# Dynamic convolution and squared-ReLU feed-forward on one core: the place of VectorE's sums of a finished chunk in each step

## The chip, the cores and the metric

The kernel runs on one core of a Trainium2 chip. The metric is the device time of one execution in microseconds (us); lower is better. TensorE does the matmuls, VectorE and ScalarE the elementwise work, SyncE issues the DMAs; GpSimd does nothing here after the start.

## The reference

Two layers, one behind the other, in fp32. The first is a convolution whose 7 weights are different at every token and head; the second is a feed-forward layer with a squared ReLU.

```python
w = softmax(weight_gen, axis=-1)            # (8, 4096, 8 heads, 7 taps)
x_pad = concat([zeros(B, 6, 192), x], axis=1)
out = einsum('bshk,bskhg->bshg', w, windows_of_7(x_pad))   # 24 channels per head
x = out.reshape(32768, 192)
h = x @ w_in                                # w_in (192, 2048), given as float64
r = maximum(h, 0.0)
return ((r * r) @ w_out).astype(float32)    # w_out (2048, 192), given as float64
```

## The kernel before

**Chunks.** Each of the 128 partitions holds 256 consecutive tokens. A chunk takes 4 of them from every partition, 512 tokens in all, so there are 64 chunks, numbered c = 0 to 63. For a chunk the convolution runs on VectorE (`conv_steps`): a softmax of six small instructions (L195 to L200, its Exp on ScalarE, L197), seven products (L211) and six additions (L216) over 128x768 tiles, and a transpose by 32x32 blocks (L270); two rounds of DMAs through DRAM (L276, L281) complete the transpose. What comes back, `xT`, is split into a high part and a low remainder (`xh` on ScalarE, L235, and `xl` on VectorE, L236), since TensorE multiplies in a shorter format; the weights `W` and `V` are stored in the same two parts.

**Steps.** A chunk passes through NJ = 8 steps, j = 0 to 7, each for 256 of the 2048 hidden columns. In a step TensorE runs `mm1(c, j)` (L296: 18 matmuls of 64 rows, in nine pairs on the two halves of the array), which fills two PSUM banks `ph`. ScalarE takes them with a ReLU (L314), squares in place (L318), and makes the high part `gh` (L322, `high`); VectorE makes the low part `gl` (L326, `low`). Then `mm2_turned` (L370: 10 matmuls for each of the two blocks, 20 in a step) adds them into four PSUM banks `acc0` to `acc3`. It runs LAG = 2 steps behind: TensorE's row in step (c, j) is `mm1(c, j)` and then the second product of two steps earlier. So the last blocks of chunk c-1 are added in step (c, 1), and in step (c, 2) the second product of chunk c begins and writes the same four banks: `ph` has four banks, `acc` the other four, and there is no second set.

**The sums.** Two banks hold the two row halves of one result. `sum_turned` takes the banks out: ScalarE copies `acc2` and `acc0` to SBUF (L378), and VectorE adds `acc3` and `acc1` to the copies (L380, two instructions), and a DMA (L381) moves a part between partitions. Only then may TensorE write the banks again. `store_turned`, in steps 5 and 6 of the same chunk, transposes the result (L389, L391, L392) and sends it out (L398, L403).

**What sets the order.** The order on every engine is that in which the Python code emits instructions. In a step the loop emits: `mm1`, `mm2_turned`, ReLUs and squares; then `late`, the two `low` instructions of the step before; then the list `todo` for this step, in which the convolution of the chunk after the next has been laid out; then `store_turned`; then, if a chunk has just been finished (`done`), `sum_turned`; then the two `high`. `plan_conv` fills `todo`: from step (m-2, 3) on, the 20 items of chunk m's convolution are spread over eight steps (`spread`), so that three of them (an addition, a product, an addition) fall into step (m-1, 1), the step of the sums. For chunk 2 alone the 14 items behind the softmax all fall into step (1, 0). The last chunk, c = 63, has no convolution beside it. It still takes out chunk 62's sums in its step 1, and its own second product runs at the end in another form (L343).

Of the kernel before, what the change touches and what calls it, by code (L numbers as in the profile page):

```python
# [19 lines left out]
def kernel(  # L20
# [27 lines left out]
    NJ = NF // 2  # L48
# [4 lines left out]
    CONV_BEG = 3  # L53
# [30 lines left out]
    def load_group(gi):  # L84
        t0 = gi * TG
        xt = xin.tile([P, TG + HALO, D], F32, name="xt")
        wt = xin.tile([P, TG, H, K], F32, name="wt")
        x_tiles[gi], w_tiles[gi] = xt, wt
        wf = wt.rearrange("p t h k -> p t (h k)")
        if gi > 0:  # L90
            nc.sync.dma_start(out=wf, in_=wg_v[:, t0:t0 + TG, :])
            nc.sync.dma_start(out=xt, in_=x_v[:, t0 - HALO:t0 + TG, :])
            return
        nc.gpsimd.memset(xt[:, 0:HALO, :], 0.0)
        nc.sync.dma_start(out=wf[:, 0:TC, :], in_=wg_v[:, 0:TC, :])
        nc.sync.dma_start(out=xt[:, HALO:HALO + TC, :], in_=x_v[:, 0:TC, :])
        for p0 in range(0, P, PPB):
            nc.sync.dma_start(
                out=xt[p0 + 1:p0 + PPB, 0:HALO, :],
                in_=x_v[p0:p0 + PPB - 1, R - HALO:R, :],  # L100
            )
# [186 lines left out]
    def mm1(c, j):  # L288
        xh, xl = xts[c]["h"], xts[c]["l"]
        two = [ps_h.tile([P, N], F32, name="ph") for _ in range(2)]  # L290
        seq = [(q, xx, k) for q, xx in ((0, xh), (0, xl), (1, xh)) for k in range(ND)]
        for n, (q, xx, k) in enumerate(seq):
            for i in range(2):
                rows = slice(i * D1, (i + 1) * D1)
                w = W[rows, q, j, k * P:(k + 1) * P]
                nc.tensor.matmul(two[i], w, xx[rows, k], start=(n == 0), stop=(n == len(seq) - 1))  # L296
        for i in range(2):
            phs[c, 2 * j + i] = two[i]

    def relu(c, fb):  # L300
        ph = phs.pop((c, fb))
        if c == 0:
            r = gp.tile([P, N], F32, name="gh" if fb < NBUF else "gl")
        else:
            r = gp.tile([P, N], F32, name="rg")
        rgs[c, fb] = r
        if c == NCH - 1:
            nc.scalar.activation(
                r.rearrange("p (t q j) -> p t q j", q=P // Q, j=Q),
                ph.rearrange("p (q t j) -> p t q j", q=P // Q, j=Q),  # L310
                AF.Relu,
            )
        else:
            nc.scalar.activation(r, ph, AF.Relu)  # L314

    def square(c, fb):
        r = rgs[c, fb]
        nc.scalar.activation(r, r, AF.Square)  # L318

    def high(c, fb):  # L320
        gh = ghs[c, fb] = gp.tile([P, N], F32R, name="gh")
        nc.scalar.copy(gh, rgs[c, fb])  # L322
# [33 lines left out]
    def mm2_turned(c, fb):  # L356
        if fb == 0:
            accs[c] = [ps_o.tile([P, N], F32, name=f"acc{t}") for t in range(4)]
        gh, gl = ghs.pop((c, fb)), gls.pop((c, fb))
        j, i = divmod(fb, 2)  # L360
        first, last = fb == 0, fb == NF - 1
        A, B = [(0, 0, gh), (0, 0, gl), (0, 1, gh)], [(2, None, gh), (2, None, gl)]
        seq = B + A if last or first else A + B
        for n, (b, q, g) in enumerate(seq):
            k = sum(1 for m in seq[:n] if m[0] == b)
            for h in range(2):
                rows = slice(h * D1, (h + 1) * D1)
                w = V[rows, fb, P:2 * P] if q is None else V[rows, fb, 2 * P * q:2 * P * q + P]
                fl = dict(start=first and k == 0, stop=last and k == (2 if b == 0 else 1))
                nc.tensor.matmul(accs[c][b + h], w, g[rows], **fl)  # L370
# [3 lines left out]
    def sum_turned(c):  # L374
        acc = accs[c]
        X = works[c] = stage.tile([P, 3, N], F32, name="raw")
        for k, b in ((1, 2), (0, 0)):
            nc.scalar.copy(X[:, k], acc[b])  # L378
        for k, b in ((1, 2), (0, 0)):
            nc.vector.tensor_tensor(out=X[:, k], in0=acc[b + 1], in1=X[:, k], op=ALU.add)  # L380
        nc.sync.dma_start(out=X[0:D1, 2], in_=X[D1:P, 1])  # L381

    def store_turned(c, part):
        X = works[c]
        if part == 0:
            o_sb = op.tile([P, TC, D], F32, name="o_sb", bufs=2)
            Y = stage.tile([P, 2, N], F32, name="raw")
            outs[c] = o_sb, Y
            nc.vector.transpose(Y[:, 0], X[:, 0])  # L389
        else:  # L390
            nc.vector.tensor_tensor(out=X[0:D1, 1], in0=X[0:D1, 1], in1=X[0:D1, 2], op=ALU.add)  # L391
            nc.vector.transpose(outs[c][1][0:D1, 1], X[0:D1, 1])  # L392
        o_sb, Y = outs[c]
        y = Y[:, part].rearrange("p (t q i) -> p q t i" if c < N_PE else "p (q t i) -> p q t i", t=TC, i=Q)
        for e in range(P // Q if part == 0 else D1 // Q):
            d0 = part * P + e * Q
            for q in range(P // Q):
                nc.sync.dma_start(  # L398
                    out=o_sb[q * Q:(q + 1) * Q, :, d0:d0 + Q],
                    in_=y[e * Q:(e + 1) * Q, q],  # L400
                )
        if part:
            nc.sync.dma_start(out=out_v[:, c * TC:(c + 1) * TC, :], in_=o_sb)  # L403
# [3 lines left out]
    def finish(c, t):  # L407
        if c not in outs:
            o_sb = op.tile([P, TC, D], F32, name="o_sb", bufs=2)
            outs[c] = o_sb, stage.tile([P, TC, 2 * D], F32, name="raw") if c > 0 else None  # L410
        o_sb, tmp = outs[c]
        acc = accs[c][t]
        if c == 0:
            nc.scalar.copy(o_sb[:, t, :], acc[:, 0:D])
        else:
            nc.scalar.copy(tmp[:, t, :], acc[:, 0:2 * D])

    def store(c, t0, t1):
        o_sb, tmp = outs[c]
        tsl = slice(t0, t1)  # L420
        if c > 0:
            for h, l in ((slice(0, P), slice(2 * P, 2 * D)), (slice(P, D), slice(D, 2 * P))):
                nc.vector.tensor_tensor(out=o_sb[:, tsl, h], in0=tmp[:, tsl, h], in1=tmp[:, tsl, l], op=ALU.add)
        nc.sync.dma_start(out=out_v[:, c * TC + t0:c * TC + t1, :], in_=o_sb[:, tsl])
# [70 lines left out]
    def at(c, j, f):  # L495
        todo.setdefault((c + j // NJ, j % NJ), []).append(f)

    def spread(fs, c, j0, j1):
        for i, f in enumerate(fs):
            at(c, j0 + (j1 - j0) * i // len(fs), f)  # L500

    def plan_conv(m, a, b):
        spread(a, max(m - 2, 1), CONV_BEG if m > 2 else 0, CONV_BEG + (NJ if m > 2 else 0))
        for f in b:
            at(m - 1, NJ - 2, f)

# [4 lines left out]
    for c in range(1, NCH):  # L511
        tail = c == NCH - 1
        for j in range(NJ):
            if j == 0 and c % 2 and (c + 3) // 2 * CPG < NCH:
                load_group((c + 3) // 2)
            if j == CONV_BEG and c + 2 < NCH:
                plan_conv(c + 2, *conv_steps(c + 2, 0))
            if c == 1 and j == 0:
                for t in range(TC):
                    finish(0, t)  # L520
                store(0, 0, TC)
            mm1(c, j)
            fbs = (2 * j, 2 * j + 1)
            done = None
            if len(pend) == LAG or tail and pend:
                c2, j2 = pend.pop(0)
                for fb in (2 * j2, 2 * j2 + 1):
                    mm2_turned(c2, fb)
                done = c2 if j2 == NJ - 1 else None
            for fb in fbs:  # L530
                relu(c, fb)
            for fb in fbs:
                square(c, fb)
            if not tail:
                pend.append((c, j))
            for f in late:
                f()
            late.clear()
            for f in todo.pop((c, j), []):
                f()  # L540
            if c > 1 and j == OUT_STEP:
                store_turned(c - 1, 0)
            if c > 1 and j == OUT_STEP + 1:
                store_turned(c - 1, 1)
            if done is not None:
                sum_turned(done)
            if not tail or j < NJ // 2:
                for fb in fbs:
                    high(c, fb)
                    late.append(lambda c=c, fb=fb: low(c, fb))  # L550
# [44 lines left out]
```

## Time and profile before

| what | value |
|---|---|
| time, median of 3 runs | 2361.75 us (2361.68 to 2362.22) |
| the profiled execution's own time | 2361.66 us |
| its span in the profile | 2359.9 us |
| TensorE matmul busy | 2255.2 us |
| VectorE busy | 1872.7 us |
| ScalarE busy | 1792.9 us |
| DMA queue 1, share of 16 engines | 32.0% |
| granted TensorE clock | 1.00 |

The span is the stretch that the profile sees; the execution's own time is 1.76 us longer. In the views, PE is TensorE's matmul side, PEld its weight loads, DVE VectorE, ACT ScalarE and SPq SyncE's queue. A row of the timeline gives the start, the length, the engine, the line, the operation with output<-input, how many instructions were merged into the row (x2: two back to back), and in brackets how long the engine had been idle before it and what ended that. A row of the waits gives the total, the number and the longest. The chain of waits follows the work back from the last instruction to what released it, and so shows which engine sets the time at each moment.

### The profile page before, as it was taken

To read this page: it belongs to the slowest core of one execution; us is meant where nothing else is said; L and a number is where in the kernel's file an instruction comes from. 1 tells how busy PE (TensorE), PEld (TensorE's weight loads), DVE (VectorE), ACT (ScalarE), POOL (GpSimd) and SP (SyncE) were. 2 spreads that over 40 slices of the span, in tenths; PEclk is the share of its full clock that TensorE was granted. 3 is DMA by queue.
4 is the path that set the end of the run, shared out by engine and by line. 5 is a ranking of instruction groups with operands and counts; after the bars stand their busy time and mean duration, and the time that the engine had idled before them with its cause. 6 is when DMAs were issued, how large, how long until landed. Compare 5 with 4: busy or idle time off the path is not lost.

```text
span 2359.9 us, 50238 instructions
## 1 busy us (share of the span) xinstructions
PE 2255.2 (96%) x19632; PEld 1837.4 (78%) x19632; DVE 1872.7 (79%) x2834; ACT 1792.9 (76%) x3462; POOL 1.7 (0%) x7
## 2 busy tenths in 40 slices
PE   7999999999999999999999999999999999999999
PEld 7777777777777777777777777777777777777777
DVE  8978878778788787787887877878878778788784
ACT  5677877777778777777787777777877777778776
POOL 0000000000000000000000000000000000000000
PEclk9999999999999999999999999999999999999999
DMA  5233233333232332333323333323333233332322
GB/s 162 59 87 95 57 82 84 83 94 80 60 96 77 89 85 55 94 81 87 96 59 80 88 80 94 81 60 95 78 89 85 56 94 80 87 95 60 80 57 50
DMA packets 321390, 191.78 MB, mean 81 GB/s; under 512 B 223752, under 2 KB 280968, under 8 KB 317184
## 3 DMA queue, kind: packets, MB, share of 16 engines
q1 hardware_dynamic: 321152, 188.58, 32.0%
q8 instruction: 153, 2.51, 0.5%
q14 instruction: 85, 0.70, 0.1%
HBM read 106.39 MB, written 49.55 MB: 66 GB/s over the span
## 4 chain that ended last, share of the span: by engine, by line
PE 93%; DVE 5%; ACT 1%; issue 0%; DMA 0%; SPq 0%; DVEq 0%; ACTq 0%
PE acc L370 48%; PE ph L296 42%; DVE pr L216 3%; DVE raw L380 2%; PE acc L334 1%; PE acc L343 1%; PE ph L253 1%; DVE pr L211 0%; DVE gl L326 0%; DMA xt<-in_x_dram 0%; ACT rg L318 0%; ACT gh L322 0%; ACT rg L314 0%; DMA raw<-in_moe_w_in_dram 0%; ACT gh L314 0%
## 5 line engine op out<-in xcount | busy, mean ns | idle before, releaser
L370 PE MATMUL acc<-gh,V 64*128 64x512 f32 x5952 | 1239.1, 388 | 85.6 <-DVE raw L380 85.6
L370 PE MATMUL acc<-gl,V 64*128 64x512 f32 x3968 | 1133.2, 390 | 2.6 <-DVE gl L326 2.6
L370 PEld LDWEIGHTS acc<-gh,V 64*128 64x128 f32 x5952 | 912.8, 184 | 243.2 <-DVE raw L380 129.7
L296 PE MATMUL ph<-xh,W 64*128 64x512 f32 x6144 | 1078.8, 386 | 2.9 <-DVE W L156 1.4
L314 ACT ACTIVATE rg<-ph 128x512 f32<-128x512 f32 x992 | 539.5, 596 | 512.8 <-PE ph L296 512.8
L326 DVE TENSOR_TENSOR gl<-rg,gh 128x512 fp32r<-128x512 f32 x1008 | 643.6, 677 | 265.6 <-ACT gh L322 265.6
L296 PEld LDWEIGHTS ph<-xh,W 64*128 64x128 f32 x6144 | 752.3, 184 | 126.6 <-ACT W L148 2.5
L370 PEld LDWEIGHTS acc<-gl,V 64*128 64x128 f32 x3968 | 715.0, 184 | 77.1 <-DVE gl L326 3.9
L318 ACT ACTIVATE rg<-rg 128x512 f32<-128x512 f32 x1008 | 582.0, 634 | 0.0
L322 ACT CAST gh<-rg 128x512 fp32r<-128x512 f32 x1008 | 576.4, 627 | 2.6 <-PE acc L343 2.6
L296 PE MATMUL ph<-xl,W 64*128 64x512 f32 x3072 | 540.1, 386 | 0.0
L296 PEld LDWEIGHTS ph<-xl,W 64*128 64x128 f32 x3072 | 376.8, 184 | 60.7 <-DVE xl L236 0.4
L211 DVE TENSOR_TENSOR pr<-xt,wt 128x768 f32<-128x768 f32 x448 | 419.1, 948 | 3.3 <-DMA xt<-in_x_dram 1.0
L216 DVE TENSOR_TENSOR pr<-pr 128x768 f32<-128x768 f32 x381 | 360.0, 945 | 0.3
L236 DVE TENSOR_TENSOR xl<-xT,xh 128x512 fp32r<-128x512 f32 x186 | 117.6, 687 | 185.2 <-ACT xh L235 185.2
L235 ACT CAST xh<-xT 128x512 fp32r<-128x512 f32 x186 | 103.0, 626 | 0.0
L380 DVE TENSOR_TENSOR raw<-acc,raw 128x512 f32<-128x512 f32 x124 | 78.9, 673 | 3.0 <-ACT raw L378 3.0
L378 ACT COPY raw<-acc 128x512 f32<-128x512 f32 x124 | 66.3, 595 | 0.0
L270 DVE STREAM_TRANSPOSE xr<-pr 128x768 f32<-128x768 f32 x62 | 60.7, 979 | 2.1
L392 DVE STREAM_TRANSPOSE raw<-raw 64x512 f32<-64x512 f32 x62 | 43.9, 709 | 2.1
L389 DVE STREAM_TRANSPOSE raw<-raw 128x512 f32<-128x512 f32 x62 | 43.7, 704 | 0.0
L391 DVE TENSOR_TENSOR raw<-raw 64x512 f32<-64x512 f32 x62 | 42.0, 677 | 0.0
(46 smaller groups left out, 377.1 us busy)
## 6 DMA issues: line engine op xcount, KB each, us to landing
xT<-xd SPq DMA_DIRECT2D x124, 384.0 KB, 4.9
xt<-in_x_dram SPq DMA_DIRECT2D x31, 1344.0 KB, 6.9
out_dram<-o_sb SPq DMA_DIRECT2D x63, 384.0 KB, 2.4
xd<-xr SPq DMA_DIRECT2D x248, 96.0 KB, 2.0
o_sb<-raw SPq DMA_DIRECT2D x1488, 16.0 KB, 1.8
raw<-raw SPq DMA_DIRECT2D x62, 128.0 KB, 2.5
wt<-in_weight_gen_dram SPq DMA_DIRECT2D x31, 224.0 KB, 3.3
raw<-in_moe_w_in_dram SPq DMA_DIRECT2D x16, 192.0 KB, 4.5
```

Source lines behind the costliest of these rows:

```text
L211: tt(out=dst, in0=src, in1=wk.broadcast_to([P, n, G]), op=ALU.mult)
L216: tt(out=prs[k0], in0=prs[k0], in1=prs.pop(k), op=ALU.add)
L235: nc.scalar.copy(xh, src[k])
L236: tt(out=xl, in0=src[k], in1=xh.bitcast(F32), op=ALU.subtract)
L296: nc.tensor.matmul(two[i], w, xx[rows, k], start=(n == 0), stop=(n == len(seq) - 1))
L314: nc.scalar.activation(r, ph, AF.Relu)
L318: nc.scalar.activation(r, r, AF.Square)
L322: nc.scalar.copy(gh, rgs[c, fb])
L326: nc.vector.tensor_tensor(out=gl, in0=rgs.pop((c, fb)), in1=ghs[c, fb].bitcast(F32), op=ALU.subtract)
L370: nc.tensor.matmul(accs[c][b + h], w, g[rows], **fl)
L378: nc.scalar.copy(X[:, k], acc[b])
L380: nc.vector.tensor_tensor(out=X[:, k], in0=acc[b + 1], in1=X[:, k], op=ALU.add)
```

## The change

Two places of the code change. `sum_turned(done)` is called behind `late` and ahead of the `todo` list, where it stood behind the list and the stores. And the 14 items of chunk 2's convolution are spread over steps (1, 0) to (1, 3), where all stood in step (1, 0).

```diff
     def plan_conv(m, a, b):
-        spread(a, max(m - 2, 1), CONV_BEG if m > 2 else 0, CONV_BEG + (NJ if m > 2 else 0))
+        if m > 2:
+            spread(a, m - 2, CONV_BEG, CONV_BEG + NJ)
+        else:
+            spread(a, 1, 0, NJ // 2)
...
             for f in late:
                 f()
             late.clear()
+            if done is not None:
+                sum_turned(done)
             for f in todo.pop((c, j), []):
                 f()
...
                 store_turned(c - 1, 1)
-            if done is not None:
-                sum_turned(done)
```

The first place, on VectorE, is step (2, 1), the first step with sums; every later chunk to 62 repeats it. `gl<-rg,gh` are the two `low`, `pr` the products and additions of the convolution, `raw<-acc` the sums. Before:

```order
118 L326 TENSOR_TENSOR gl<-rg,gh 128x512 x2
119 L216 TENSOR_TENSOR pr<-pr 128x768
120 L211 TENSOR_TENSOR pr<-xt,wt 128x768
121 L216 TENSOR_TENSOR pr<-pr 128x768
122 L380 TENSOR_TENSOR raw<-acc_800,raw 128x512
123 L380 TENSOR_TENSOR raw<-acc_798,raw 128x512
124 L326 TENSOR_TENSOR gl<-rg,gh 128x512 x2
125 L216 TENSOR_TENSOR pr<-pr 128x768
```

The same place with the change:

```order
118 L326 TENSOR_TENSOR gl<-rg,gh 128x512 x2
119 L380 TENSOR_TENSOR raw<-acc_796,raw 128x512
120 L380 TENSOR_TENSOR raw<-acc_794,raw 128x512
121 L216 TENSOR_TENSOR pr<-pr 128x768
122 L211 TENSOR_TENSOR pr<-xt,wt 128x768
123 L216 TENSOR_TENSOR pr<-pr 128x768
124 L326 TENSOR_TENSOR gl<-rg,gh 128x512 x2
125 L216 TENSOR_TENSOR pr<-pr 128x768
```

The two sums have passed three instructions of the convolution; what stands ahead of and behind the five is as it was. (The numbers behind `acc` only count tiles.)

The second place, on VectorE, is steps (1, 0) to (1, 3), where chunk 2's convolution is laid out anew; `xr<-pr` is its transpose, and `mx`, `wt` begin chunk 3's softmax. Before:

```order
81 L326 TENSOR_TENSOR gl<-rg,gh 128x512 x2
82 L216 TENSOR_TENSOR pr<-pr 128x768
83 L211 TENSOR_TENSOR pr<-xt,wt 128x768
...
88 L211 TENSOR_TENSOR pr<-xt,wt 128x768
89 L216 TENSOR_TENSOR pr<-pr 128x768 x2
90 L270 STREAM_TRANSPOSE xr<-pr 128x4x6x32
91 L156 TENSOR_TENSOR V<-du,V 128x4x128
92 L156 TENSOR_TENSOR V<-du,V 128x4x64
93 L326 TENSOR_TENSOR gl<-rg,gh 128x512 x2
94 L195 TENSOR_REDUCE mx<-wt 128x32
95 L196 TENSOR_TENSOR wt<-wt,mx 128x224
```

The same place with the change:

```order
80 L326 TENSOR_TENSOR gl<-rg,gh 128x512 x2
81 L211 TENSOR_TENSOR pr<-xt,wt 128x768
...
88 L211 TENSOR_TENSOR pr<-xt,wt 128x768
89 L156 TENSOR_TENSOR V<-du,V 128x4x128
90 L156 TENSOR_TENSOR V<-du,V 128x4x64
91 L326 TENSOR_TENSOR gl<-rg,gh 128x512 x2
92 L216 TENSOR_TENSOR pr<-pr 128x768 x2
93 L270 STREAM_TRANSPOSE xr<-pr 128x4x6x32
94 L195 TENSOR_REDUCE mx<-wt 128x32
95 L196 TENSOR_TENSOR wt<-wt,mx 128x224
```

The `low` instructions and the two of `V` come earlier among the convolution's; the instructions ahead of row 94 are the same ones on both sides.

## The prediction

> **What bounds the kernel now.** I read the waits first: which engine stands still, and for whom. The columns are the total in us, the number of waits and the longest.
>
> ```profile
> PE acc L370 <- DVE raw L380: 85.6, 61, 1.4
> PE acc L370 <- DVE gl L326: 2.6, 3, 1.3
> DVE gl L326 <- ACT gh L322: 265.6, 194, 5.9
> ```
>
> TensorE has one wait that repeats: 61 times it stands before the second product until VectorE's sums are done. Beside it stand only three waits for `gl`, at the start. VectorE itself waits for ScalarE, much longer in total, but that is slack. Next the chain of waits through one chunk (start, length, what), which shows what the wait consists of.
>
> ```profile
> 1012.87 2.04 PE ph L296 x18
> 1014.91 2.27 PE acc L370 x20
> 1017.17 1.84 PE ph L296 x17
> 1019.01 0.02 issue
> 1019.03 0.94 DVE pr L216
> 1019.97 0.61 DVE raw L380
> 1020.58 0.04 issue
> 1020.62 2.70 PE acc L370 x19
> 1023.33 2.04 PE ph L296 x18
> ```
>
> Step 1 is 2.04 + 2.27 us of TensorE. In step 2 the first product ends, and the chain goes over to VectorE: an addition of the convolution, then the first sum, then TensorE goes on. The price of it comes from the busy time by stretches (length, PE busy, PEld busy and so on): steps 7 to 1 as three, step 2 by itself, and the next six.
>
> ```profile
> 1003.65:1016.57 12.92, 12.92 (x118) 10.68 (x116) 12.07 (x17) 10.91 (x22) 0.00 (x0) 1.00 0.16 25
> 1016.57:1022.72 6.15, 4.74 (x42) 3.40 (x39) 6.15 (x10) 5.43 (x11) 0.00 (x0) 1.00 0.72 235
> 1022.72:1048.56 25.84, 25.84 (x232) 21.36 (x229) 18.58 (x30) 19.33 (x38) 0.00 (x0) 1.00 0.36 86
> ```
>
> An undisturbed step takes 12.92 / 3 = 25.84 / 6 = 4.307 us, with TensorE never idle and its clock granted at 1.00; the step with the sums takes 6.15, that is 1.843 more. The longest list of the chain confirms it over the whole run:
>
> ```profile
> 113.13 2.70 PE acc L370 x19
> 2182.22 2.70 PE acc L370 x19
> ```
>
> These two are 57 chunks apart, (2182.22 - 113.13) / 57 = 36.30 us a chunk, and 36.30 - 8 x 4.307 = 1.845. So TensorE is the bound in seven steps of eight, and in the eighth VectorE's queue is.
>
> **The change, first part: the sums pass three convolution instructions.** Here is VectorE from the `low` pair ahead of that step's convolution to the pair behind it, and TensorE's and ScalarE's rows that matter beside them.
>
> ```profile
> 1016.09 1.28 DVE L326 TENSOR_TENSOR gl<-rg,gh 128x512 fp32r<-128x512 f32 x2
> 1017.29 0.94 DVE L216 TENSOR_TENSOR pr<-pr 128x768 f32<-128x768 f32 x1
> 1019.90 1.27 DVE L380 TENSOR_TENSOR raw<-acc,raw 128x512 f32<-128x512 f32 x2
> 1021.10 1.27 DVE L326 TENSOR_TENSOR gl<-rg,gh 128x512 fp32r<-128x512 f32 x2
> 1016.74 1.07 ACT L378 COPY raw<-acc 128x512 f32<-128x512 f32 x2
> 1018.61 0.18 PEld L370 LDWEIGHTS acc<-gh,V 64*128 64x128 f32 x1
> 1020.62 0.50 PE L370 MATMUL acc<-gh,V 64*128 64x512 f32 x1 [1.41 <-DVE raw L380]
> ```
>
> The three instructions between the `low` pair and the sums take 1019.90 - 1017.29 = 2.61 us. ScalarE's two copies, which the sums need, run from 1016.74 to 1017.81; the first is done about 1017.33. So with the change VectorE begins the sums at 1017.3 to 1017.4 with almost no wait, and they end at about 1018.0 and 1018.65 (1.27 us for two). TensorE's first weights for the new chunk load at 1018.61, its second matmul needs the first sum at about 1018.7, and the second sum's bank is needed two pairs of matmuls later, 0.45 us on (20 matmuls, ten pairs, take 2.27 us). Spare: about 0.65 us for the first, 0.4 to 0.5 for the second. The whole 1.845 should go.
>
> The program has this case without the convolution already, once: in its last chunk nothing else stands in front of the sums.
>
> ```profile
> 2323.59 1.06 PE L296 MATMUL ph<-xh,W 64*128 64x512 f32 x6
> 2323.53 1.07 ACT L378 COPY raw<-acc 128x512 f32<-128x512 f32 x2
> 2324.15 1.29 DVE L380 TENSOR_TENSOR raw<-acc,raw 128x512 f32<-128x512 f32 x2 [2.98 <-ACT raw L378]
> ```
>
> The first sum starts 0.62 us after the copies do, one copy later, and both are over 2324.15 + 1.29 - 2323.59 = 1.85 us after the step's first matmul. A first product lasts 2.04 us. So taking the banks out fits under it, if VectorE is free.
>
> The Trainium skill, page "Perfetto Trace Analysis", section "Optimization Strategy", reads such a gap another way: the same gap repeating on the engine that should be saturated can mean that there isn't enough PSUM for the next tile. The kernel has indeed no second set of accumulator banks; by that rule an order on VectorE would not help and the time would stay. The last chunk's row speaks against it here: one set is enough.
>
> What is queued behind the sums now: the three convolution instructions, 1.27 us later, and then the `low` pair at 1021.10, whose place does not move, since the same five instructions stand ahead of it. But TensorE will be 1.845 us earlier against VectorE from there on. That pair is used in step 3's second product, which began at 1022.72 + 2.04 = 1024.76 and will begin at 1022.92; its first half is done at about 1021.75. Cover remains: over 1 us. The lead is then eaten by VectorE's waits, in the next four steps:
>
> ```profile
> 1028.13 1.29 DVE L326 TENSOR_TENSOR gl<-rg,gh 128x512 fp32r<-128x512 f32 x2 [1.98 <-ACT gh L322]
> 1032.15 1.29 DVE L326 TENSOR_TENSOR gl<-rg,gh 128x512 fp32r<-128x512 f32 x2 [1.83 <-ACT gh L322]
> 1040.77 1.90 DVE L236 TENSOR_TENSOR xl<-xT,xh 128x512 fp32r<-128x512 f32 x3 [3.01 <-ACT xh L235]
> ```
>
> They are 6.8 us, so 1.845 can be taken out of them and VectorE still waits for ScalarE at step 6, as today. From there to the sums it stands against TensorE as it does today. The next thing to be late would be the `low` pair of step 6:
>
> ```profile
> 1009.37 1.24 DVE L326 TENSOR_TENSOR gl<-rg,gh 128x512 fp32r<-128x512 f32 x2
> 1010.22 0.41 PEld L370 LDWEIGHTS acc<-gl,V 64*128 64x128 f32 x2
> ```
>
> Its first half is done at about 1010.0 and used at 1010.22. It is in time today, and it is bound to the step 6 wait, which stays. ScalarE's order is unchanged. It will reach the Exp (L197) of step 3 earlier than VectorE delivers for it and wait a little there; TensorE does not feel that, since `ph` has four banks and `mm1` writes two. SyncE's order is unchanged too: the sums' DMA (L381) is ready some 2.5 us sooner and its consumer (L391) is in step 6. The transposed block of the convolution is sent out at the same moment while its use in step 6 comes 1.845 sooner:
>
> ```profile
> 1029.99 1.28 SPq L281 DMA_DIRECT2D xT<-xd  x2
> 1040.12 1.66 ACT L235 CAST xh<-xT 128x512 fp32r<-128x512 f32 x3
> xT<-xd SPq DMA_DIRECT2D x124, 384.0 KB, 4.9
> ```
>
> The last of it is issued at about 1031.3 and lands 4.9 us later, at 1036.2; the use moves to 1038.3. Cost nothing, 2 us of cover.
>
> **Second part: chunk 2's convolution is spread.** Cost by instructions: none added. What it may free are TensorE's three waits for `gl`, 2.6 us. What limits it is ScalarE: its queue stands at the Exp of chunk 3 until VectorE has done all of chunk 2's convolution, and that work ahead of L196 is the same.
>
> ```profile
> 87.26 0.39 ACT L197 ACTIVATE wt<-wt 128x224 f32<-128x224 f32 x1 [6.10 <-DVE wt L196]
> 101.83 1.29 DVE L326 TENSOR_TENSOR gl<-rg,gh 128x512 fp32r<-128x512 f32 x2
> 103.32 0.39 PE L370 MATMUL acc<-gl,V 64*128 64x512 f32 x2
> 113.13 0.50 PE L370 MATMUL acc<-gh,V 64*128 64x512 f32 x1 [1.04 <-DVE raw L380]
> ```
>
> ScalarE goes on at 87.26 either way, with the work of the 6.10 us before still to do, so the `low` pair at 101.83 stays where it is; its first half ends at about 102.5, and TensorE uses it at 103.32. TensorE can therefore come forward by 0.8 us at most there. I take 0.8. The ends are 0 (a new wait eats it) and about 3.5 (all three waits and the loads lost with them go, if ScalarE's pause should shrink).
>
> **The sum.** Sixty waits of 1.845 are 110.7. The first of the 61 is shorter by 1.41 - 1.04 = 0.37, so 1.47. The start gives 0.8. Together 113.0. Against the profiled execution's 2361.66 (its span 2359.9 and 1.76 around it; the median of the runs is 0.09 above it) that is 2248.7 us. Ends: all of the start's 3.5 and a wait-free rest give 2246.0, and 1 us below for what the rows round away 2245. If VectorE came to the sums one convolution instruction late (0.87, a third of 2.61), 0.87 - 0.65 = 0.22 would be left of every wait, 13.4 us in all, 2262.
>
> **The rivals.**
>
> *VectorE's lag is carried round.* If the 1.845 us of lead were not eaten by VectorE's waits, the `low` pair of step 6, with 0.2 us to spare, would be late by about 1.6 in each of 61 chunks: 100 us come back, 2349. Between that and my forecast lie all partial cases (a part of the lag carried, 0.3 to 1.5 us per chunk). For it: the margin of 0.2 is the smallest I found, and VectorE is busy 29.0 of what will be 34.45 us. Against it: 6.8 us of waits per chunk. 8%.
>
> ```profile
> 1000.00:1036.30 36.30, 34.89 (x306) 28.32 (x304) 29.04 (x44) 27.91 (x55) 0.00 (x0) 1.00 0.40 104
> ```
>
> *The banks are the limit.* The four banks must be emptied by ScalarE and VectorE in series, whatever stands in the queue. If emptying them took 3.9 us from the first product's start instead of 1.85, the wait would stay: 2361, no change. The last chunk's row excludes this unless the copies come late in mid-run; there they start at 1016.74, as early in the step as at the end. 2%. (This is what the sentence of the Trainium skill's page "Perfetto Trace Analysis" would mean here.)
>
> *Slower.* The sums now wait at the head of VectorE's queue for ScalarE's copies, and the convolution and the next `low` pair wait behind them. In the last chunk that wait was 2.98 us, since VectorE had nothing else. In mid-run VectorE arrives when the first copy is done. If ScalarE fell behind so that the copies came X later, the `low` pair for step 3 would be late by X - 1.3 (used at 1022.92 + 0.22, done at 1021.75), and from X = 3.2 on the loss outweighs the 1.845; at X = 4.5 each chunk loses 3.2 - 1.845 = 1.36, 83 us, 2445. ScalarE has a wait for TensorE in nearly every step, so I see no way to it. 3%.
>
> **How the numbers follow.** The forecast has 87%, the carried lag and its partial cases 8%, no change 2%, slower 3%. A measurement of this kernel can tell 0.2%, 4.7 us, from no change. Nearly all partial cases are faster by more than that: faster 0.95, within 0.2% 0.02, slower 0.03. The range is the forecast's own, 2245 to 2263; what it leaves out are the rivals, 13%, and the rarer tail of the start.
>
> **What would show it.** In the profile after, TensorE's waits for L380 should be gone or near it (below 5 us for 85.6); chunks should follow each other every 34.45 us; VectorE's row of the sums should stand ahead of L216 with an idle time under 0.2 us; its waits at the three rows above should sum to about 5 us; the chain should be TensorE for over 97%. I am wrong if TensorE shows a new wait that repeats 61 times: for `gl` (the first rival), for L380 still (the second), or if VectorE's wait for L378 reaches several us per chunk (the third).

## The result, and the profile after

The changed kernel takes 2248.66 us (median of 4 runs, 2248.49 to 2248.87) against 2361.97 us before (4 runs, one more than in the table above, 2361.68 to 2362.22): a ratio of 0.952, with a 95% interval of 0.9504 to 0.9537, 113.3 us less. The two profiled executions stand at 2361.66 and 2248.87 us, 112.8 apart.

First the busy times of the whole span (the page's first part).

```profile
span 2247.1 us, 50238 instructions
PE 2228.5 (99%) x19632; PEld 1846.3 (82%) x19632; DVE 1877.8 (84%) x2834; ACT 1798.7 (80%) x3462; POOL 1.7 (0%) x7
```

Busy time and instructions of VectorE and ScalarE are the same as before within 0.4%; only the span has shrunk around them. In the chain that ended last, TensorE had 93% of the span before; after, it is nearly all of it:

```profile
PE 97%; DVE 1%; ACT 1%; DMA 0%; issue 0%; SPq 0%; DVEq 0%; ACTq 0%
```

What VectorE and TensorE wait for, after:

```profile
DVE gl L326 <- ACT gh L322: 147.5, 193, 5.9
DVE raw L380 <- ACT raw L378: 3.0, 1, 3.0
PEld acc L370 <- DVE gl L326: 2.1, 3, 0.8
PEld acc L370 <- ACT gh L322: 1.1, 1, 1.1
PE acc L370 <- DVE gl L326: 1.0, 3, 0.4
PE acc L370 <- ACT gh L322: 0.7, 1, 0.7
```

TensorE's row for L380 (85.6 us in 61 waits) is gone altogether. The waits of VectorE's `low` instructions for ScalarE have given up 265.6 - 147.5 = 118 us: that is where the time was taken from. The one wait of the sums that is left, 3.0 us, is the last chunk's, as before. Next one chunk by stretches: the whole of it, step 1, step 2, and the other six.

```profile
965.90:1000.36 34.46, 34.46 (x308) 28.48 (x305) 29.13 (x45) 28.02 (x55) 0.00 (x0) 1.00 0.41 109
965.90:970.21 4.31, 4.31 (x41) 3.56 (x38) 4.31 (x7) 3.16 (x7) 0.00 (x0) 1.00 0.15 23
970.21:974.52 4.31, 4.31 (x42) 3.56 (x39) 4.31 (x7) 4.13 (x9) 0.00 (x0) 1.00 0.68 211
974.52:1000.36 25.84, 25.84 (x232) 21.36 (x229) 20.51 (x33) 20.73 (x41) 0.00 (x0) 1.00 0.41 107
```

Step 2, which took 6.15 us, is now a step like any other, and TensorE is busy for the whole of the 34.46 us. VectorE around the sums, and its waits up to step 6:

```profile
969.72 1.28 DVE L326 TENSOR_TENSOR gl<-rg,gh 128x512 fp32r<-128x512 f32 x2
971.00 1.29 DVE L380 TENSOR_TENSOR raw<-acc,raw 128x512 f32<-128x512 f32 x2
972.20 0.95 DVE L216 TENSOR_TENSOR pr<-pr 128x768 f32<-128x768 f32 x1
...
974.81 1.29 DVE L326 TENSOR_TENSOR gl<-rg,gh 128x512 fp32r<-128x512 f32 x2
...
980.84 1.29 DVE L326 TENSOR_TENSOR gl<-rg,gh 128x512 fp32r<-128x512 f32 x2 [0.97 <-ACT gh L322]
...
983.95 1.29 DVE L326 TENSOR_TENSOR gl<-rg,gh 128x512 fp32r<-128x512 f32 x2 [0.92 <-ACT gh L322]
...
992.56 1.90 DVE L236 TENSOR_TENSOR xl<-xT,xh 128x512 fp32r<-128x512 f32 x3 [3.01 <-ACT xh L235]
```

The sums follow the `low` pair with no idle time noted, and the convolution follows them. (They begin 1.28 us behind the pair, while the instruction behind the sums begins 1.20 us after them: some 0.08 us are a wait too short for the view to note.) The three waits that were 1.98, 1.83 and 3.01 are 0.97, 0.92 and 3.01: the first two have paid, together 1.92 us, and the third has not been touched.

### The profile page after: what moved, and what is told of

Same layout as the page of the kernel before. It is cut to its first block, busy times and chain, and to the rows that moved or that the text cites. A ratio compares the mean times of both kernels' runs of the same rounds, so it can differ in the third digit from the quotient of the medians.

```text
span 2247.1 us, 50238 instructions
## 1 busy us (share of the span) xinstructions
PE 2228.5 (99%) x19632; PEld 1846.3 (82%) x19632; DVE 1877.8 (84%) x2834; ACT 1798.7 (80%) x3462; POOL 1.7 (0%) x7
## 4 chain that ended last, share of the span: by engine, by line
PE 97%; DVE 1%; ACT 1%; DMA 0%; issue 0%; SPq 0%; DVEq 0%; ACTq 0%
PE acc L370 49%; PE ph L296 45%; PE acc L334 1%; PE acc L343 1%; PE ph L253 0%; DVE pr L211 0%; DVE pr L216 0%; DMA xt<-in_x_dram 0%; ACT rg L318 0%; ACT gh L322 0%; DVE gl L326 0%; DVE V L156 0%; DMA raw<-in_moe_w_in_dram 0%; ACT rg L314 0%; ACT gh L314 0%
## 5 line engine op out<-in xcount | busy, mean ns | idle before, releaser
L370 PE MATMUL acc<-gh,V 64*128 64x512 f32 x5952 | 1007.5, 386 | 0.7 <-ACT gh L322 0.7
L296 PE MATMUL ph<-xh,W 64*128 64x512 f32 x6144 | 863.9, 386 | 3.0 <-DVE W L156 1.4
L370 PE MATMUL acc<-gl,V 64*128 64x512 f32 x3968 | 772.8, 386 | 1.0 <-DVE gl L326 1.0
L326 DVE TENSOR_TENSOR gl<-rg,gh 128x512 fp32r<-128x512 f32 x1008 | 644.1, 678 | 147.6 <-ACT gh L322 147.5
L296 PEld LDWEIGHTS ph<-xh,W 64*128 64x128 f32 x6144 | 575.8, 184 | 126.9 <-ACT W L148 2.7
L370 PEld LDWEIGHTS acc<-gh,V 64*128 64x128 f32 x5952 | 557.5, 184 | 118.1 <-ACT gh L322 1.1
L370 PEld LDWEIGHTS acc<-gl,V 64*128 64x128 f32 x3968 | 371.7, 184 | 80.1 <-DVE gl L326 2.1
L296 PE MATMUL ph<-xl,W 64*128 64x512 f32 x3072 | 432.3, 386 | 0.0
L296 PEld LDWEIGHTS ph<-xl,W 64*128 64x128 f32 x3072 | 288.3, 184 | 60.8 <-DVE xl L236 0.4
L380 DVE TENSOR_TENSOR raw<-acc,raw 128x512 f32<-128x512 f32 x124 | 79.9, 687 | 3.0 <-ACT raw L378 3.0
L197 ACT ACTIVATE wt<-wt 128x224 f32<-128x224 f32 x64 | 25.1, 392 | 68.3 <-DVE wt L196 68.3
```

The lines of the kernel that those rows point to most:

```text
L326: nc.vector.tensor_tensor(out=gl, in0=rgs.pop((c, fb)), in1=ghs[c, fb].bitcast(F32), op=ALU.subtract)
```

## The experiments

All kernels but one are the changed kernel with an edit. A ratio is to the kernel before, run beside the kernel named. A cost per chunk below is the difference to the changed kernel's 2248.66 us over 61 chunks. In the kernels with a scratch tile the lines are one higher (L371 is L370, L381 is L380).

**Each part alone.** The first keeps only the sums in front and spreads chunk 2's convolution as before:

```diff
     def plan_conv(m, a, b):
-        if m > 2:
-            spread(a, m - 2, CONV_BEG, CONV_BEG + NJ)
-        else:
-            spread(a, 1, 0, NJ // 2)
+        spread(a, max(m - 2, 1), CONV_BEG if m > 2 else 0, CONV_BEG + (NJ if m > 2 else 0))
```

> Only the sums are moved; chunk 2's convolution stands in step (1, 0) as before. Queue theory (the three convolution instructions ahead of the sums were the wait, the spreading is worth the start alone): about 0.6 us above the changed kernel, which came forward by 0.57 us at the start, so 2249.2 us. Rival (the spreading is needed for the gain, since VectorE would otherwise enter the main loop with a lag that it carries from chunk to chunk): waits for L380 or gl come back in many chunks, 2260 us or more.

Measured: 2248.97 us (2248.90 to 2249.20), ratio 0.9524, 0.9511 to 0.9537. The second keeps only the spreading: the kernel before with the other half of the diff.

> Only chunk 2's convolution is spread over steps (1, 0) to (1, 3); the sums stand behind the convolution as before. Queue theory: 61 waits for L380 as before, 0.6 us less at the start, 2361.4 us. Rival (part of the gain comes from the spreading): below 2360 us.

Measured: 2361.34 us beside 2361.53 of the kernel before, ratio 1.0002, 0.9994 to 1.0011. Its waits:

```profile
PEld acc L370 <- DVE raw L380: 130.3, 122, 2.1
PE acc L370 <- DVE raw L380: 86.2, 61, 1.7
PE acc L370 <- DVE gl L326: 1.0, 3, 0.4
```

The whole of the gain belongs to the sums. The spreading takes TensorE's waits for `gl` at the start from 2.6 to 1.0 us and is worth 0.2 to 0.3 us in the medians, which neither run can tell apart from nothing. The rival that the main loop needs it is out.

**How far in front?** The sums were put behind the first of the three convolution instructions, and behind the second:

```diff
-            if done is not None:
-                sum_turned(done)
-            for f in todo.pop((c, j), []):
+            fs = todo.pop((c, j), [])
+            if done is not None:
+                fs.insert(1, lambda: sum_turned(done))
+            for f in fs:
                 f()
```

> The sums are issued behind the first of the three convolution instructions. Queue theory with a spare of 0.65 us: the sums come 0.87 us later, 0.2 to 0.35 us of wait in each of 61 chunks, 12 to 21 us, 2261 to 2270 us. Rival (no spare: whatever delays the sums is paid in full): 0.87 x 61 = 53 us, 2302 us. Rival (the banks are the limit, not the place in the queue): no difference from the changed kernel, 2249 us.

> The sums are issued behind the second of the three convolution instructions. Queue theory: one more instruction of 0.87 us is paid in full now that the spare is used up, 53 us above the kernel with one ahead, 2314 to 2323 us. Rival (no spare): 2355 us. Rival (banks): 2249 us.

Measured: 2256.78 us with one ahead (2255.46 to 2257.78; ratio 0.9556, 0.9543 to 0.957) and 2308.61 with two (2308.52 to 2308.96; 0.9776, 0.9761 to 0.9791). With three it is the kernel that only spreads, 2361.34. So the three instructions cost 8.1, 51.8 and 52.7 us, or 0.13, 0.85 and 0.86 us per chunk. An instruction takes 0.87 us (2.61 / 3). The second and third are paid in full or nearly so, the first to 0.13: 0.74 us of it cost nothing. That excludes both rivals, no spare (53 us at once) and the banks as the limit (no cost). My expectation for the first, 12 to 21 us, failed: the measured 8.1 is a third below its lower end. I had taken the whole 0.87 us as delay of the sums, but in the changed kernel they wait some 0.08 us for ScalarE's first copy anyway, so they come only 0.79 later, and 0.79 less my spare of 0.65 is 0.14, near the 0.13 that was measured. In the kernel with one ahead no matmul is listed as waiting for the sums. The wait is in the weight loads, and the second product of that step takes 2.40 us for 2.27:

```profile
PEld acc L370 <- DVE raw L380: 14.7, 62, 0.3
```

```profile
1011.15 2.40 PE acc L370 x20
```

**Is VectorE's idle time slack, and where?** One addition over a scratch tile was added in chunks 2 to 62, in step 4 and, in another kernel, in step 6:

```diff
+    junk = const.tile([P, TC * D], F32, name="junk")
...
+            if 1 < c < NCH - 1 and j == 4:
+                nc.vector.tensor_tensor(out=junk, in0=junk, in1=junk, op=ALU.add)
             if c > 1 and j == OUT_STEP:
                 store_turned(c - 1, 0)
```

> One more VectorE addition over a scratch tile of 128x768 (0.87 us from start to start) in step 4 of chunks 2 to 62, behind the convolution's share. Queue theory: VectorE waits 0.92 us for ScalarE right behind it in the changed kernel, and 3 us more up to step 6, so it costs nothing, 2248.7 us. Rival (VectorE's lag is carried round, its waits are no slack): up to 0.87 x 61 = 53 us, 2302 us.

> The same added instruction in step 6, between the splits and the low pair that TensorE uses 0.24 us after it is ready. Queue theory: the place counts, not the amount; 0.87 - 0.24 = 0.63 us in each of 61 chunks, 38 us, 2287 us, with a new wait of TensorE for gl (L326). Rival (VectorE has room anywhere, 5 us per chunk): 2248.7 us.

Measured: 2248.35 us in step 4 (2248.27 to 2249.11), nothing; 2285.73 us in step 6 (2285.48 to 2286.13; ratio 0.9678, 0.9663 to 0.9692), 37.1 us or 0.61 per chunk. The row of step 4, with the wait behind it that was 0.92 us and has vanished:

```profile
1016.87 0.89 DVE L549 TENSOR_TENSOR junk<-junk 128x768 f32<-128x768 f32 x1
1017.87 1.29 DVE L327 TENSOR_TENSOR gl<-rg,gh 128x512 fp32r<-128x512 f32 x2
```

And step 6: VectorE's added instruction and the `low` pair, and TensorE's weight load that waits for that pair, a wait that the changed kernel doesn't have in the main loop.

```profile
1011.69 0.95 DVE L549 TENSOR_TENSOR junk<-junk 128x768 f32<-128x768 f32 x1
...
1013.90 1.24 DVE L327 TENSOR_TENSOR gl<-rg,gh 128x512 fp32r<-128x512 f32 x2
```

```profile
1014.60 0.19 PEld L371 LDWEIGHTS acc<-gl,V 64*128 64x128 f32 x2 [0.74 <-DVE gl L327]
```

```profile
PEld acc L371 <- DVE gl L327: 46.6, 63, 0.8
```

The same 0.87 us of work costs nothing in one step and 0.61 in another, though VectorE is idle about 5 us in each chunk: the lag is not carried round, it is absorbed at the next wait, but between the splits and that `low` pair there is no wait. The spare there is 0.87 - 0.61 = 0.26 us.

**Does waiting at the head of the queue cost?** ScalarE got one, then two copies over a scratch tile in front of its copies of the banks, so that the sums wait at the head of VectorE's queue with the convolution and the next `low` pair behind them:

```diff
             if done is not None:
+                if not tail:
+                    for _ in range(1):
+                        nc.scalar.copy(junk, junk)
                 sum_turned(done)
```

> One more ScalarE copy over a scratch tile of 128x512 (0.52 us from start to start) ahead of the two copies of the accumulators in chunks 2 to 62, so the sums wait 0.5 us at the head of VectorE's queue. Queue theory: inside the spare of 0.5 to 0.7 us, 0 to 5 us, 2249 to 2254 us. Rival (waiting at the head of the queue is dear, since the convolution and the next low pairs wait behind): 0.5 x 61 = 32 us, 2280 us.

> Two such copies, 1.04 us. Queue theory: 0.35 to 0.55 us beyond the spare in each of 61 chunks, 21 to 34 us, 2270 to 2283 us, shown as waits of TensorE for L380, not for gl, since the low pair behind has over 1 us of cover. Rival (the head of the queue is dear): 63 us or more, 2312 us, with waits for gl too.

Measured: 2248.36 us with one (2248.20 to 2249.11) and 2279.10 with two (2279.01 to 2279.32; ratio 0.965, 0.9634 to 0.9666), 0 and 30.4 us, 0.50 per chunk. The row of the sums with one copy:

```profile
1005.46 1.29 DVE L381 TENSOR_TENSOR raw<-acc,raw 128x512 f32<-128x512 f32 x2 [0.52 <-ACT raw L379]
```

With two, the idle time and the waits:

```profile
1019.65 1.29 DVE L381 TENSOR_TENSOR raw<-acc,raw 128x512 f32<-128x512 f32 x2 [1.17 <-ACT raw L379]
```

```profile
DVE raw L381 <- ACT raw L379: 73.9, 62, 3.0
PEld acc L371 <- DVE raw L381: 47.5, 122, 0.5
PEld acc L371 <- DVE gl L327: 2.1, 3, 0.8
```

With one copy VectorE stands still for half a us in every chunk and TensorE feels nothing. With two it stands still for 1.17 us and 0.50 is paid, so 0.67 is spare; the wait is for the sums alone, and the wait for `gl` remains the start's three. What the third rival said, a late `low` pair behind the waiting sums, doesn't show up to this delay; a longer one was not run.

**What of the start is left?** In step (1, 3) ScalarE stands 6.07 us before chunk 3's Exp. The softmax's first instructions were put in front of the rest of chunk 2's convolution:

```diff
             if j == CONV_BEG and c + 2 < NCH:
+                left = todo.pop((c, j), []) if c == 1 else []
                 plan_conv(c + 2, *conv_steps(c + 2, 0))
+                if left:
+                    todo[c, j] += left
```

> The changed kernel, with one order in step (1, 3) turned round: chunk 3's first softmax instructions (L195, L196, and the Exp) ahead of the last three instructions of chunk 2's convolution. Queue theory: ScalarE's wait of 6.07 us for L196 ends 2.8 us sooner, TensorE's waits of 0.73 for gh and 0.42 for gl in the first chunk go and about 0.3 for gl is left: 1 us below the changed kernel, 2247.6 us. Rival (the start is bound elsewhere): 2248.7 us.

> The changed kernel again, on the chip of the run before it, as its measure: 2248.7 us by every theory.

Measured: 2250.73 us (ratio 0.9522, 0.9509 to 0.9535; four runs: 2250.70, 2250.89, 2250.75 and 2248.97) against 2248.63 of the changed kernel on the same chip (2248.56 to 2248.83; 0.9515, 0.9502 to 0.9528). My expectation failed. The rival's holds in one run (2248.97); in the other three something comes on top. ScalarE's row in the changed kernel, and then its rows here:

```profile
87.29 0.39 ACT L197 ACTIVATE wt<-wt 128x224 f32<-128x224 f32 x1 [6.07 <-DVE wt L196]
```

```profile
84.32 0.39 ACT L197 ACTIVATE wt<-wt 128x224 f32<-128x224 f32 x1 [3.23 <-DVE wt L196]
97.01 1.66 ACT L235 CAST xh<-xT 128x512 fp32r<-128x512 f32 x3 [2.69 <-DMA xT<-xd]
```

The Exp comes 2.97 us sooner, and ScalarE loses 2.69 of it again later, at chunk 2's transposed block on its way through DRAM. That DMA had not shown as a wait before, because ScalarE used to arrive late. The edit also moves the transpose itself back, behind the softmax's instructions: VectorE begins it at 86.18 us, and at 85.35 in the changed kernel on the same chip. TensorE then waits once for longer than before:

```profile
102.90 0.49 PE L370 MATMUL acc<-gl,V 64*128 64x512 f32 x2 [1.85 <-DVE gl L326]
```

What follows that wait is told in the last section.

## Why the prediction was right

*The term of the sums.* 60 x 1.845 + 1.47 was to go, and it went: no wait for L380 is left, and a chunk takes 34.46 us where 34.45 was worked out. The two estimates that it rested on were tested apart. The first was that the three instructions are the wait: put back one by one they cost 0.13, 0.85 and 0.86 us, together 1.84. The second was that emptying the banks fits under the first product: the last chunk's row had said so, and the kernel with the sums alone shows it for every chunk. The signs that I had named came too: no wait for L380, no idle time noted before the sums, 0.97 + 0.92 + 3.01 = 4.90 us for the three waits, and no new wait of TensorE that repeats. TensorE has 97% of the chain, where I had asked for over 97.

*The spare.* I had 0.65 us from rows of three engines. The runs give 0.66 by the queue (0.87 - 0.13, less the 0.08 us that the sums wait anyway) and 0.67 by ScalarE (1.17 - 0.50), so it was read rightly. The bound that I built on it, 13.4 us for one instruction late, measured 8.1: the 0.08 us was missing in it.

*The carried lag.* It did not come, for the reason given: VectorE's two waits in steps 4 and 5 paid 1.92 us and the wait before the splits stayed at 3.01. The place that I named as next to be late, the `low` pair of step 6 with 0.2 us, is next: its spare is 0.26 us.

*ScalarE at the Exp.* That it would wait there, unnoticed by TensorE, is the one new wait in the main loop, 0.8 us in a chunk:

```profile
979.90 0.39 ACT L197 ACTIVATE wt<-wt 128x224 f32<-128x224 f32 x1 [0.80 <-DVE wt L196]
```

*The start.* I took 0.8 us, and TensorE was 0.57 us further on when it reached the first wait for the sums (the first product of that step began at 109.67 before and at 109.10 after). The `low` pair at 101.83 stayed where it was, at 101.86, which was the argument. TensorE used it at 102.60 and not at 102.5. The matmuls from there to the next first product then took 2.19 us (102.60 to 104.79), where they had taken 2.04 (103.32 to 105.36). They stand right behind a wait; why they are slower there was not tested.

*The rule of the Trainium skill, page "Perfetto Trace Analysis".* The gap did repeat on the engine that should be saturated, and the accumulators did have one set of banks only. But it was not for lack of PSUM: with the same four banks the gap is gone.

The sum hit the median to a tenth of a us, which is partly luck: the start was 0.2 us short, and the step lengths are read to 0.01 us and multiplied by 60.

## What to carry to other kernels

When one engine waits at regular intervals for another that is far from full, look at what stands in the other's queue between the moment the input is ready and the instruction waited for; work without a deadline belongs behind it. A place in the program where the same instruction runs with an empty queue (here the last chunk) tells beforehand whether the chain itself fits. And idle time in total says nothing on where work can be put: the spare has to be read at each deadline, from the last wait before it.

## What the runs showed of the hardware

One thing I had not expected. In the kernel of the start, and in the profiled run of the one that only spreads (2363.38 us, where its median is 2361.34), TensorE's granted clock fell to half after a single gap of under two us, and stayed there about 3.4 us. The first, by stretches; the PE columns first, the clock third from the right:

```profile
102.00:103.00 1.00, 0.10 (x2) 0.11 (x2) 1.00 (x3) 1.00 (x3) 0.00 (x0) 1.00 0.00 0
103.00:104.00 1.00, 1.00 (x8) 0.81 (x10) 1.00 (x2) 1.00 (x3) 0.00 (x0) 0.79 0.00 0
104.00:105.00 1.00, 1.00 (x6) 0.77 (x6) 1.00 (x2) 1.00 (x3) 0.00 (x0) 0.50 0.00 0
...
106.00:107.00 1.00, 1.00 (x8) 0.81 (x6) 1.00 (x3) 0.00 (x0) 0.00 (x0) 0.50 0.00 0
107.00:108.00 1.00, 1.00 (x10) 0.83 (x10) 1.00 (x2) 0.00 (x0) 0.00 (x0) 1.00 0.00 0
```

The gap, from the end of the matmul before to the next at 102.90, shows 1.85 us of idle time. In the other kernel it was 1.65:

```profile
113.23 0.50 PE L370 MATMUL acc<-gh,V 64*128 64x512 f32 x1 [1.65 <-DVE raw L380]
```

```profile
114.00:115.00 1.00, 1.00 (x8) 0.82 (x10) 1.00 (x3) 0.54 (x2) 0.00 (x0) 0.81 0.62 133
115.00:116.00 1.00, 1.00 (x8) 0.76 (x6) 0.96 (x2) 0.00 (x0) 0.00 (x0) 0.50 0.03 6
...
118.00:119.00 1.00, 1.00 (x12) 0.79 (x10) 0.71 (x3) 0.00 (x0) 0.00 (x0) 0.98 0.93 198
```

The 61 regular waits of the kernel before are 1.41 us at most in the same view, with the clock at 1.00 throughout. The Trainium skill, page "TensorE: Matmul & The Clock Gate", section "Why this matters for your kernels", advises against idle gaps of more than about 3 us. In these two runs a gap of under 2 was followed by the half clock.

It does not happen in every run. Of the first kernel's four runs, three have a mean clock of 0.999 (2250.70 to 2250.89 us) and one has 1.000 (2248.97); of the other's eleven, four have 0.999 (2362.78 to 2364.07) and seven 1.000 (2361.22 to 2361.38). The times at which the clock changes, as the traces record them, suggest why: in these two traces the half clock lasts 3.413 us, and the stretches of full clock before and after it last 26 and 627 times as much in the first kernel (88.75 and 2140.16 us), 29 and 657 times in the other (98.99 and 2242.56 us). The half clock began at 103.58 and at 114.62 us, and the gap lay inside the 3.413 us before that both times. So the clock seems to be set once in each such stretch, and whether a gap of this size counts may hang on whether it falls into one stretch or into two. That is an inference: there is no trace of a run of these two kernels without the drop, and I made no run to find the length at which it begins. At half the clock 3.4 us lose 1.7, which is near the 1.7 and 2.0 us by which these executions were longer (2250.70 - 2248.97, 2363.38 - 2361.34); that is read from two traces, not tested.
